# Three pairs' attention scores in row tile 7 instead of 5, and a reordered load queue in row tile 3

## The chip, the core and the metric

The kernel runs on one core of one Trainium2 chip. The core has five instruction queues that run side by side: PE (TensorE, the matrix unit), DVE (VectorE), ACT (ScalarE), POOL (GpSimd) and SP (SyncE, which here only issues DMAs). They meet through semaphores. Matmul results go to PSUM, an accumulator memory of eight banks, from which DVE and ACT read. The metric is device microseconds (us) of one execution; less is better.

## The reference

Inputs q, k and v have 8 batches, 8 heads, 576 positions and 64 values per head. The first half is a retention layer: attention without softmax, with a causal decay that depends on the head.

```
gamma_h = 1 - 2 ** (-5 - h)
ret = (q @ k.T / sqrt(64)) * (gamma_h ** (i - j) where i >= j, else 0)
x   = (ret @ v), heads side by side        # 4608 rows x 512
```

The second half is a two-layer feed-forward on these 4608 rows:

```
h   = x @ w_in                             # 512 -> 2048
g   = h * cos(h)
out = g @ w_out                            # 2048 -> 512
```

## The kernel before

**Pairs and tiles.** The 4608 rows are cut into 18 *pairs* of 256 rows (numbered G) for the retention, and into ten *row tiles* (numbered n) for the feed-forward: one of 512 rows, two of 256, then seven of 512. From tile 3 on (`S7 = 3`) tile n reads the retention results of pairs 2n-2 and 2n-1. The retention of later pairs is laid between the matmuls of the current tile, so that PE always has something to do.

**Retention of one pair.** The decay is split into a factor on q and one on k, applied when they are cast to bf16: `prep_q` and `prep_k` (line 179; `quad` calls `prep_q` four times), nearly always on POOL. `turn_q` and `turn_k` (line 205) then transpose the results by a DMA that SP issues; `turned`, `turned_q` call them. v is only cast: `values` on ACT (line 816) or in `early` on POOL. On PE a pair has five groups of matmuls, 64 x 64 x 64 each from pair 6 on:

- *scores* (`scores`, line 286): 32 matmuls kT x qT, into banks "a"; DVE multiplies them by the causal mask (line 298) and writes `ret`
- *cross* and *same* (line 469, out<-qT,sb): 16 each, the queries times the running state of all earlier positions
- *own* (line 469, out<-ret,vb): 32, the masked scores times v
- *states* (`states`, line 359): k times v; DVE adds them to the running state (lines 380, 382), ACT casts it (lines 390, 391)

cross, own and same add into the same PSUM bank, from which ACT and DVE copy the rows x, transposed, to `xT` (line 494). cross and own use other rows of the matrix unit on the same bank, so after cross a switch is put: `run("cross", True)` appends `nc.scalar.nop()`, an empty instruction on ACT that waits for the last cross matmul, and the first own matmul waits for it.

**A row tile from 3 on** has two halves. In the first, `mm1` (line 545) makes h in eight blocks, ACT takes the cosine (line 553) and DVE the product g (line 554). In the second, `mm2_seven` makes the output with seven products of half-size blocks in the place of eight (the Strassen-like scheme), in the order x = 3, 4, 5, 2, 1, 7, 6, each of 16 matmuls of 128 x 128 x 256 (line 697). Five of the products need sums of parts of g, `g_sum` (line 624), which `sums_after` and `late_sums` hand to DVE or POOL. A POOL sum that follows a DVE sum waits for it. Results are added on DVE (line 722), copied by ACT (lines 742, 747, 752) and stored by `store` (line 729), which then calls `feed`: it issues the next loads and preparations.

**Where the retention sits.** `mm2_seven(n, at)` runs `at[x]` ahead of product x. There are two arrangements:

- tiles 3, 4 and 5, three places: ahead of 5, scores and states of the next pair (`at_once(*ready(G))`); ahead of 1, `unit(G)`: cross of G, scores of G+1, own and same of G, states of G+1; ahead of 6, `begin(G + 1)` and `end(both)`: cross, own and same of G+1 with nothing between. In tile 5 the last place is a `unit` too, which takes the scores and states of the pair after that: three pairs' scores in one tile.
- tiles 6 and 7, two places: a `unit` ahead of 4 and one ahead of 1.

So tiles 3 to 5 take their pairs' scores in the tile itself, and from the end of tile 5 on they are taken one place ahead. Tile 8 ends the retention; tile 9 has none.

**Order.** The program order of each queue is the order in which the Python code emits (the schedule is manual), and each queue runs in that order: what stands behind a waiting instruction waits as well. SP issues nearly all loads, transposes and stores through one queue. Around the change, `feed` in tile 3 is called by the stores of that tile: with r = 0 after the first (`c12`), r = 1 after the second (`c21`), r = 2 and r = 3 after the last two. The first is emitted ahead of product 2, the second ahead of product 1.

Of the kernel before, what the change touches and what calls it, by code (L numbers as in the profile page):

```python
# [17 lines left out]
def kernel(  # L18
# [39 lines left out]
    assert sum(widths) == NTOK  # L58
    starts = [sum(widths[:n]) for n in range(len(widths))]
    S7 = 3  # L60
    LD = 3

    consts = ctx.enter_context(tc.tile_pool(name="consts", bufs=1))
# [346 lines left out]
    def retention(G, bank="m", evac=nc.scalar.copy):  # L410
# [52 lines left out]
        def run(name, switch=False):  # L463
            i = None
            for h, x, yq, n, lhsT, rhs in parts.pop(name):
                at = (x, h % 2)
                left[at] -= 1
                dst = outs[x][half(h % 2), yq, h // 2, :n]
                i = nc.tensor.matmul(  # L469
                    dst if name == "own" else as_queries(G, dst),  # L470
                    lhsT=lhsT,
                    rhs=rhs,
                    start=at not in begun,
                    stop=left[at] == 0,
                    skip_group_check=True,
                )
                begun.add(at)
                if turn:
                    fence(i, turn.pop(), "other rows")
            if switch and i is not None:  # L480
                turn.append(nc.scalar.nop())
                fence(turn[0], i, "other rows")

        def done(*evacs):
# [121 lines left out]
    def g_sum(n, x, e0, e1):  # L606

        gT = tiles["g", n]
        a, b, op_ = {
            5: ((0, 0), (0, 1), ALU.add),  # L610
            2: ((1, 0), (1, 1), ALU.add),
            1: ((0, 0), (1, 1), ALU.add),
            7: ((0, 1), (1, 1), ALU.subtract),
            6: ((1, 0), (0, 0), ALU.subtract),
        }[x]
        if ("gs", n, x) not in tiles:
            tiles["gs", n, x] = sump.tile([P, E2, 256], BF16, tag=f"gs{x}", name=f"gs{x}")
        i0, i1 = (
            gT[:, k * E2 + e0 : k * E2 + e1, r * 256 : (r + 1) * 256] for r, k in (a, b)
        )  # L620
        on_dve = x == 5 or (n, x) == (S7, 2) or (n, x, e0) in (
            (S7, 1, 4), (S7 + 1, 2, 4), (S7 + 2, 2, 4), (last, 1, 0), (last, 2, 4)
        ) or (x == 6 and e0 == 0 and S7 < n < last)
        i = (nc.vector if on_dve else nc.gpsimd).tensor_tensor(  # L624
            out=tiles["gs", n, x][:, e0:e1], in0=i0, in1=i1, op=op_
        )
        if on_dve:
            tiles["gate"] = i
        elif "gate" in tiles:
            fence(i, tiles.pop("gate"), "port free")  # L630

    def sums_after(n, i):

        if n == S7:
            if i < 4:
                w_sums(3 + i % 2, i // 2 * 4, i // 2 * 4 + 4)
            elif i < 6:
                g_sum(n, 5, i % 4 * 4, i % 4 * 4 + 4)
                if i == 5:
                    g_sum(n, 6, 0, 4)  # L640
            elif i == 7:
                g_sum(n, 2, 0, E2)
                g_sum(n, 1, 4, E2)
                g_sum(n, 1, 0, 4)
                for e in (0, 4):
                    g_sum(n, 7, e, e + 4)
                g_sum(n, 6, 4, E2)
        elif n in (S7 + 1, S7 + 2) and i in (3, 7):
            for x in (5, 2):
                g_sum(n, x, i - 3, i + 1)  # L650
            if i == 7:
                g_sum(n, 6, 0, 4)
            g_sum(n, 1, i - 3, i + 1)
            if i == 7:
                for e in (0, 4):
                    g_sum(n, 7, e, e + 4)
                g_sum(n, 6, 4, E2)
        elif i == 3:
            for x in (5, 2, 1, 7) if n < last else (5, 1, 2, 7, 6):
                g_sum(n, x, 0, 4)  # L660
        elif i == 7 and n == last:
            late_sums(n)
# [111 lines left out]

    open_, stores = [], []

    def begin(G, bank="m"):
        run, done = retention(G, bank)
        run("cross", True)
        open_.append(lambda *evacs: (run("own"), run("same"), done(*evacs)))  # L780

    def end(evacs=()):
# [18 lines left out]
    def turned(G):  # L801
        if G < FINE:
            turn_q(G // 2, G % 2)
        turn_k(G)
# [13 lines left out]
    def feed(s):  # L818
# [3 lines left out]
        if n == 0:  # L822
            if r == 0:
                load_q(5)
                load(10)
            elif r == 2:
                quad(4)
                turned_q(4)
                prep_k(8, 0)
                prep_k(8, 1)  # L830
                turned(8)
            elif r == 3:
                prep_k(9, 0)
                prep_k(9, 1)
                turned(9)
                values(8)
                values(9)
            return
# [216 lines left out]
    for n, w in enumerate(widths):  # L1055
# [66 lines left out]
            ]  # L1122
        else:
            at = {}
            if n in (3, 4, 5):
                at = {
                    5: lambda acts, flush, later: (flush(), at_once(*ready(G))),
                    1: lambda acts, flush, later: unit(G, acts, flush),
                    6: lambda acts, flush, later: (flush(), begin(G + 1), end(both)),
                }  # L1130
                if n == 5:
                    at[6] = lambda acts, flush, later: unit(
                        G + 1, acts, flush, lambda masks, add, copy: (masks[0](), add(), copy())
                    )
# [62 lines left out]
```

## Time and profile before

| what | value |
|---|---|
| median of 4 runs | 297.25 us (294.71, 295.07, 299.43, 299.59) |
| the profiled execution, its own time | 294.71 us |
| its span, first to last instruction | 292.9 us |
| PE busy | 279.0 us (95%) |
| DVE, POOL, ACT busy | 207.6, 182.6, 148.9 us |
| granted TensorE clock | 1.00 in every stage |
| DMA, bytes moved | 50.39 MB |

The profile is that of one execution. An engine's busy time says how much it did, not whether it set the end; for that the chain of work that ended last is followed back from the last instruction, and it runs on PE for 88% of the span. In these answers "issue" is time in which an engine waited for nothing that the profile shows. PE's matmuls overlap and their ends are modelled, so durations of stages are taken from starts: from the first matmul of one stage to the first of the next.

### The profile page before, as it was taken

Reading aid. Unit: us, or ns where it says so; the run is one execution under the profiler, and the core shown is the slowest. Engines: PE = TensorE matmul, PEld = TensorE weight load, DVE = VectorE, ACT = ScalarE, POOL = GpSimd, SP = SyncE. Lnnn points to the kernel's source line nnn. Section 1 sums busy time; section 2 is a strip of 40 time slices with the busy share of each in tenths; the row PEclk is TensorE's granted clock in tenths of the full one; section 3 lists DMA queues with packets and bytes.
Section 4 is the critical chain, followed back from the end, with each engine's and each line's share of the span. In section 5 each row is a group of like instructions: output and inputs, shape, how many; then the busy total and the mean of one; then the engine's idle time right before and its main releaser. Section 6 shows DMA issues by size and latency. Waiting matters only on the chain.

```text
span 292.9 us, 8814 instructions
## 1 busy us (share of the span) xinstructions
PE 279.0 (95%) x3822; PEld 192.5 (66%) x3845; DVE 207.6 (71%) x267; ACT 148.9 (51%) x198; POOL 182.6 (62%) x160
## 2 busy tenths in 40 slices
PE   7779999999999999999999979999999999999995
PEld 2658745847658887458745865488548844884594
DVE  6665765494848988589758976788479848945873
ACT  5446614634426636664466436756474657525620
POOL 7890038571194269997686694399949914860583
PEclk9999999999999999999999999999999999999999
DMA  7999999999999999998999999919992240021013
GB/s 223 267 173 190 220 261 242 179 284 239 202 207 209 212 207 232 216 191 192 199 223 224 209 217 223 195 25 258 225 216 41 74 110 0 4 96 50 0 38 108
DMA packets 119031, 50.39 MB, mean 172 GB/s; under 512 B 83024, under 2 KB 117968, under 8 KB 118992
## 3 DMA queue, kind: packets, MB, share of 16 engines
q1 hardware_dynamic: 114224, 45.10, 75.8%
q0 software_dynamic: 4224, 4.19, 9.0%
q8 instruction: 30, 0.49, 0.7%
q10 hardware_dynamic: 544, 0.52, 0.5%
q14 instruction: 9, 0.07, 0.1%
HBM read 36.70 MB, written 9.44 MB: 158 GB/s over the span
## 4 chain that ended last, share of the span: by engine, by line
PE 88%; DVE 6%; issue 2%; ACT 2%; POOL 1%; DVEq 0%; ACTq 0%; POOLq 0%
PE h L545 42%; PE o L697 27%; PE o L562 9%; PE ov L469 4%; PE sc L286 2%; PE st L359 2%; PE tr L985 1%; DVE ret L302 1%; DVE xT L494 1%; DVE ot L722 1%; DVE s L382 1%; ACT kT L241 1%; ACT sb L391 0%; DVE ret L298 0%; DVE qs L974 0%
## 5 line engine op out<-in xcount | busy, mean ns | idle before, releaser
L624 POOL TENSOR_TENSOR gs<-gT 128x1024 bf16<-128x1024 bf16 x44 | 92.4, 2131 | 60.2 <-DVE gs L624 33.5
L545 PE MATMUL h<-xT,w_in_sb 128*128 128x256 bf16 (+1 forms) x756 | 126.7, 325 | 2.2 <-DVE xT L494 1.3
L554 DVE TENSOR_TENSOR gT<-h,cosh 128x1024 bf16<-128x1024 f32 x72 | 87.9, 1223 | 46.9 <-ACT cosh L553 46.5
L553 ACT ACTIVATE cosh<-h,half_pi 128x1024 f32<-128x1024 f32 x72 | 80.2, 1114 | 56.1 <-PE h L545 56.1
L545 PEld LDWEIGHTS <-w_in_sb 128*128 128x128 bf16 x768 | 74.5, 98 | 51.7 <-DVE xT L494 1.8
L697 PEld LDWEIGHTS <-gs 128*128 128x128 bf16 x576 | 53.8, 98 | 6.9 <-POOL gs L624 0.2
L179 POOL TENSOR_TENSOR qs<-fq,gq 128x512 bf16<-128x512 f32 x31 | 31.7, 1056 | 31.6 <-DMA fq<-in_q_dram 31.6
L179 POOL TENSOR_TENSOR ks<-fk,gk 128x512 bf16<-128x512 f32 x34 | 36.7, 1097 | 5.9 <-DMA fk<-in_k_dram 5.8
L697 PE MATMUL o<-ws,gs 128*128 128x256 bf16 (+1 forms) x352 | 38.7, 268 | 0.0
L562 PE MATMUL o<-w_out_sb,gT 128*128 128x512 bf16 x117 | 28.2, 379 | 1.1 <-issue 0.9
L494 ACT CAST xT<-ov 128x512 bf16<-128x512 f32 x28 | 16.3, 622 | 19.4 <-PE ov L469 19.3
L697 PE MATMUL o<-w_out_sb,gT 128*128 128x256 bf16 x224 | 26.1, 273 | 0.0
L722 DVE TENSOR_TENSOR ot<-o,ot 128x512 f32<-128x512 f32 (+2 forms) x32 | 19.6, 619 | 8.7 <-PE o L697 8.2
L697 PE MATMUL o<-w_out_sb,gs 128*128 128x256 bf16 x224 | 25.8, 273 | 0.0
L390 ACT CAST sb<-s 128x768 bf16<-128x768 f32 (+2 forms) x16 | 10.7, 672 | 28.8 <-DVE s L382 26.4
L697 PEld LDWEIGHTS <-gT 128*128 128x128 bf16 x224 | 21.6, 98 | 4.0
L624 DVE TENSOR_TENSOR gs<-gT 128x1024 bf16<-128x1024 bf16 (+1 forms) x25 | 21.3, 883 | 0.4
L562 PEld LDWEIGHTS <-gT 128*128 128x128 bf16 x128 | 11.5, 98 | 12.2
L722 DVE TENSOR_TENSOR ot<-ot,o 128x512 f32<-128x512 f32 x14 | 9.6, 685 | 7.4 <-ACT ot L752 6.2
L298 DVE TENSOR_TENSOR ret<-sc,tri 128x1024 bf16<-128x1024 f32 x12 | 14.6, 1213 | 0.0
L302 DVE TENSOR_TENSOR ret<-sc,tri 128x1024 bf16<-128x1024 f32 x10 | 11.9, 1218 | 2.7 <-PE sc L286 2.6
L469 PE MATMUL ov<-qT,sb 64*64 64x64 bf16 (+1 forms) x424 | 11.2, 201 | 1.2 <-ACT sb L391 0.8
(86 smaller groups left out, 194.4 us busy)
## 6 DMA issues: line engine op xcount, KB each, us to landing
out_dram<-ot SPq DMA_DIRECT2D x35, 256.0 KB, 4.0
fk<-in_k_dram SPq DMA_DIRECT2D x23, 256.0 KB, 6.8
fv<-in_v_dram SPq DMA_DIRECT2D x23, 256.0 KB, 5.2
fk<-in_k_dram SPq DMA_DIRECT2D x4, 512.0 KB, 7.6
fv<-in_v_dram SPq DMA_DIRECT2D x4, 512.0 KB, 7.4
w_in_sb<-in_moe_w_in_dram POOLq DMA_DIRECT2D x4, 512.0 KB, 6.3
w_out_sb<-in_moe_w_out_dram POOLq DMA_DIRECT2D x4, 512.0 KB, 14.1
fq<-in_q_dram SPq DMA_DIRECT2D x4, 512.0 KB, 6.9
```

The lines of the kernel that those rows point to most:

```text
L179: eng.tensor_tensor(out=out_.rearrange("p (b a) d -> p a b d", a=2), in0=f.rearrange("p (a b) d -> p a b d", a=2), in1=by.rearrange("p (a ...
L298: nc.vector.tensor_tensor(out=ret, in0=ps, in1=by, op=ALU.mult)
L302: nc.vector.tensor_tensor(out=ret.rearrange(shape, r=2), in0=ps.rearrange(shape, r=2), in1=by.unsqueeze(1).to_broadcast([P, H, P]), op=ALU ...
L469: i = nc.tensor.matmul(dst if name == "own" else as_queries(G, dst), lhsT=lhsT, rhs=rhs, start=at not in begun, stop=left[at] == 0, skip_g ...
L494: (evacs or (evac, evac))[x](xT[:, x], ps)
L545: nc.tensor.matmul(ps[:, j, :], lhsT=w_in_sb[:, dg, (et + j) * P : (et + j + 1) * P], rhs=xT[:, dg], start=(dg == 0), stop=(dg == DG - 1),)
L553: nc.scalar.activation(cosh, ps, ACTF.Sin, bias=half_pi, scale=1.0)
L554: nc.vector.tensor_mul(gT[:, et : et + m, c0 : c0 + w], ps, cosh)
L562: nc.tensor.matmul(ps, lhsT=gT[:, et, tsi * P : (tsi + 1) * P], rhs=w_out_sb[:, et, :], start=(et == 0), stop=(et == ET - 1),)
L624: i = (nc.vector if on_dve else nc.gpsimd).tensor_tensor(out=tiles["gs", n, x][:, e0:e1], in0=i0, in1=i1, op=op_)
L697: nc.tensor.matmul(dst[i], lhsT=lhs[:, e, j * P : (j + 1) * P], rhs=rhs[:, e, c0:c1], start=(x in (3, 4, 1, 7) and e == 0 and (i == 0 or l ...
L722: pend.append(lambda: nc.vector.tensor_tensor(out=out_, in0=in0, in1=in1, op=op_))
```

## The change

Tiles 6 and 7 get the three-place arrangement that tiles 3, 4 and 5 had; the tile whose last place is a `unit`, with three pairs' scores, is now 7. The sums of g in these tiles follow: product 2's second half goes to DVE. In all three-place tiles the switch between cross and own in `begin` is a drain of PE itself instead of the empty ACT instruction. And in tile 3's `feed` the load of pair 10 is split: k stays at r = 0, v comes after the second store's transposes, and the preparation of q and k of pair 8 and their transposes move from the third store to the second.

```diff
+    CATCH = 7
...
             if switch and i is not None:
-                turn.append(nc.scalar.nop())
+                turn.append(nc.tensor.drain() if switch == "here" else nc.scalar.nop())
                 fence(turn[0], i, "other rows")
...
         on_dve = x == 5 or (n, x) == (S7, 2) or (n, x, e0) in (
-            (S7, 1, 4), (S7 + 1, 2, 4), (S7 + 2, 2, 4), (last, 1, 0), (last, 2, 4)
-        ) or (x == 6 and e0 == 0 and S7 < n < last)
+            (S7, 1, 4), (last, 1, 0), (last, 2, 4)
+        ) or (x == 2 and e0 == 4 and S7 < n <= CATCH) or (x == 6 and e0 == 0 and S7 < n < last)
...
-        elif n in (S7 + 1, S7 + 2) and i in (3, 7):
+        elif n <= CATCH and i in (3, 7):
...
-    def begin(G, bank="m"):
+    def begin(G, bank="m", switch=True):
         run, done = retention(G, bank)
-        run("cross", True)
+        run("cross", switch)
...
             if r == 0:
                 load_q(5)
-                load(10)
-            elif r == 2:
+                load(10, "k")
+            elif r == 1:
                 quad(4)
                 turned_q(4)
                 prep_k(8, 0)
                 prep_k(8, 1)
                 turned(8)
+                load(10, "v")
...
-            if n in (3, 4, 5):
+            if n <= CATCH:
                 at = {
                     5: lambda acts, flush, later: (flush(), at_once(*ready(G))),
                     1: lambda acts, flush, later: unit(G, acts, flush),
-                    6: lambda acts, flush, later: (flush(), begin(G + 1), end(both)),
+                    6: lambda acts, flush, later: (
+                        flush(), begin(G + 1, switch="here"), end(both)
+                    ),
                 }
-                if n == 5:
+                if n == CATCH:
                     at[6] = lambda acts, flush, later: unit(
                         G + 1, acts, flush, lambda masks, add, copy: (masks[0](), add(), copy())
                     )
```

No instruction on PE is added or lost but the drains. By the instruction streams, SP keeps its DMAs: in tile 3 the order changes from k, v (pair 10), store, store, three transposes, store to k, store, three transposes, v, store, store. POOL loses two sums to DVE, one in tile 6 and one in tile 7, and its order in tile 3 stays as it was.

## The prediction

> **What bounds the kernel now.** I read the page first: PE is busy 279.0 of 292.9 us, so a gain must take time out of PE's stream. Then I asked for PE's waits after 85 us, where the change lies. There is a single one:
>
> ```profile
> PE ov L469 <- issue: 2.1, 1, 2.1
> ```
>
> Everything else from tile 3 to tile 9 is matmul after matmul. So a tile's time is its matmuls plus what it loses when it changes from the feed-forward to the retention and back. The chain of work that ended last, in order of time, gives the starts of the stages:
>
> ```profile
> 130.21 3.51 PE o L697 x32
> ...
> 145.73 0.22 PE h L545
> ...
> 159.54 3.49 PE o L697 x32
> ...
> 172.67 0.30 PE ov L469 x30
> 172.97 2.10 issue
> 175.07 0.29 PE ov L469 x12
> ...
> 177.50 0.22 PE h L545
> ...
> 191.32 1.75 PE o L697 x16
> ...
> 206.19 0.21 PE h L545
> ...
> 220.01 1.75 PE o L697 x16
> ...
> 234.88 0.22 PE h L545
> ```
>
> Columns are start, duration, what. From the first "o" to the next "h" is the second half of a tile, the only half that the change touches. It takes 145.73 - 130.21 = **15.52 us** in tile 4 (three places, 256 retention matmuls), 177.50 - 159.54 = **17.96** in tile 5 (three places, 320 matmuls, and the 2.10 us in which PE waited for nothing the profile shows), 206.19 - 191.32 = **14.87** in tile 6 and 234.88 - 220.01 = **14.87** in tile 7 (two places, 256 matmuls each). The first halves agree: 13.84 us in tile 4 (116.37 to 130.21), 13.82 in tiles 6 and 7.
>
> The windows over these halves say what surrounds them; the last two columns are DMA share and GB/s:
>
> ```profile
> 130.20:145.70 15.50, 15.39 (x354) 13.22 (x352) 12.80 (x20) 7.33 (x13) 10.85 (x7) 1.00 1.10 182
> 159.50:177.50 18.00, 15.90 (x418) 13.75 (x416) 14.79 (x24) 8.08 (x15) 15.51 (x12) 1.00 1.12 226
> 191.30:206.20 14.90, 14.90 (x354) 13.02 (x352) 12.50 (x18) 8.11 (x14) 14.28 (x9) 1.00 0.70 156
> 220.00:234.90 14.90, 14.90 (x354) 13.00 (x352) 12.51 (x18) 8.10 (x14) 14.28 (x9) 1.00 0.22 56
> ```
>
> The clock is 1.00 throughout, DVE and POOL have room, and DMA is saturated in tiles 4 and 5 but nearly idle in tile 7.
>
> **The change, part by part.** *Arrangement.* Tile 5 becomes what tile 4 is: 17.96 to 15.52, **-2.44**. Tile 6 becomes what tile 4 is: 14.87 to 15.52, **+0.65**. Tile 7 becomes what tile 5 was. Whether it inherits the 2.10 us is the main question; without them it takes 17.96 - 2.10 = 15.86, **+0.99**. Sum **-0.80**. The 0.65 are no extra matmuls. From tile 4's timeline, its places take 0.65 (133.73 to 134.38), 1.4 and 0.9 us for 64, 128 and 64 matmuls, against 1.2 twice for 128 in tile 6: one more change of shape, and a wait between cross and own.
>
> *Will the 2.10 us follow?* They lie within the own matmuls, 30 of which are recorded before and 2 after; only the first own matmul has a wait in the instruction stream, the others none, so no engine's result is missing. What is left is PE's own instruction supply. The page has a row for it:
>
> ```profile
> q8 instruction: 30, 0.49, 0.7%
> ```
>
> 30 packets carry 0.49 MB, 16 KB each, and 0.49 MB over PE's 7,692 instructions is 64 bytes for each, so one packet is 256 instructions. 0.7% of 16 engines' 292.9 us is 32.8 us, 1.1 us for a packet. Tile 5's second half holds the most instructions for its time: 320 retention matmuls with their weight loads are 640 instructions, two and a half packets, and they run at some 8.4 ns a matmul (0.27 us for 32). It does so with DMA at 1.12. After the change this crowd stands in tile 7, around 231 us, where DMA is at 0.22. I take the stall as gone, at two chances to one. The Trainium skill, "Runtime: NRT & Kernel Launch", section on instruction fetch mechanics, says that refills come in 16 KiB blocks of 256 instructions, as the row shows, but also that PE's instruction memory holds 2048 instructions and that the crossing is mostly hidden; that speaks against my cause, for so deep a store would not run dry in 640. By it the stall is something else and might go along: the sum would then be 2.10 higher. The page also calls this memory two blocks deep, and no run here settles which.
>
> *Drain for ACT's empty instruction*, at four places (tiles 3 to 6, ahead of product 6). In tile 4 the cross matmuls start at 142.88 and own at 143.31; in a unit, where scores stand between, 16 cross matmuls are followed after 0.26 (167.21 to 167.47). The switch thus costs 0.17 here, and 0.19 in tile 3 (113.50 to 113.95, less 0.26). A drain must still let the last cross matmul end, about 0.2 after its start (mean of one: 196 ns). The best is -0.19 at each of the four, -0.76; the trace has no drain on PE, so the upper bound comes from the nearest row of an emptied PE that starts again, a matmul's 0.2 us more at each, +0.8. The two rows nearest to it (0.17 and a 0.2 us latency) say that it nearly pays itself; I take **-0.1** and keep both ends. The Trainium skill, "PSUM — Partial Sum Buffer", section on engine vs sequencer instructions, says that a drain waits until the engine is wholly idle. By it PE would also lose the weight loads that it runs ahead, and the sum would lie nearer 294.7 than 293.8; no row here shows it.
>
> *Sums.* One POOL sum (2.13 us) becomes a DVE sum (0.88) in each of tiles 6 and 7, and POOL's first-half sum for product 7 moves behind block 7. That is tile 4's order, whose 15.52 contains it: **0**. Cover: the last POOL sum of tile 4 ended at 143.02, product 6 began at 143.9. Without that cover each us late is a us of PE. DVE's xT copy ended at 145.29 and the next h began at 145.73: 0.44 us of slack, inherited by tiles 5 and 6.
>
> *SP in tile 3.* The SP queue before:
>
> ```profile
> 113.16 1.98 SPq L170 DMA_DIRECT2D fk<-in_k_dram  x2
> 115.23 6.28 SPq L170 DMA_DIRECT2D fv<-in_v_dram  x2
> 121.61 1.75 SPq L729 DMA_DIRECT2D out_dram<-ot  x2
> 123.47 3.10 SPq L205 DMA_TRANSPOSE qT<-qs  x2
> 126.66 1.29 SPq L205 DMA_TRANSPOSE kT<-ks  x1
> ```
>
> v of pair 10 holds the queue for 6.28 us; the transposes of pair 8 come behind it, land by about 130 (3.1 to 4.8 us after issue) and are used at 133.64. Their q and k were ready on POOL at 117.5 and 119.6. After the change they go some 2 us sooner, and nobody waited for them: **0**. v then starts near 126 instead of 115: the same back-pressure of about 5 us first holds the store (to 120.3), then come store, transposes and kT (1.2 + 3.1 + 1.3). Its second half lands near 127 + 9.0 = 136; ACT casts it at 137.96. The slack is 2 us, and behind that cast stand ACT's copy of product 2 (139.00) and product 7, which needs that bank at about 141.2: 1.6 us more.
>
> *What is late next.* Before, kT of pairs 14 and 16 land at 198.9 and 227.5 (195.78 + 3.1, 224.50 + 3.0), their scores start at 199.67 and 228.4: 0.8 and 0.9 us of slack. After, scores of 14 move into tile 7 and those of 16 to its end near 231: over 20 and 3 us. The order is thus sturdier against a late DMA.
>
> **Sum.** The profiled execution took 294.71: 292.9 of span and 1.81 around it. 294.71 - 0.80 - 0.1 = **293.8**. The median of the runs shown is 297.25, 2.54 above the profiled one; the others reach 299.59. I forecast 293.8 for the median as well, because two races with under 1 us of slack go; if the scatter stays, it comes on top (rival two).
>
> **The rivals.**
> - *The stall stays*, in tile 7 or elsewhere: 293.8 + 2.1 = **295.9**. For it: no wait explains it, and the crowd of instructions is the same. Against it: DMA at 0.22 there. Chance 0.15.
> - *The scatter stays*: whatever put three runs 0.4 to 4.9 us above the profiled one is not in these tiles. 293.8 + 2.5 = **296.3**, up to 298.7. For it: half the runs lie so. Against: the slack gained. Chance 0.22.
> - *v of pair 10 comes too late* (slower than before). One place: ACT's cast at 137.96. If each transpose is held as v's first half was (5.04 us), v starts at 133 and lands at 142: 4 us past its use, 2.4 past product 7's bank, 293.8 + 2.4 = **296.2**, 1.5 over the profiled time. It decides from 3.6 us late. Against: transposes took 1.3 to 1.7 us each. Chance 0.07.
> - *The arrangement is free*: tile 4's 0.65 come from saturated DMA, not from three places. Then tile 5 takes 14.87 + 0.34, tile 6 14.87, tile 7 15.21: -2.75 + 0 + 0.34 = -2.4, and **292.2**. Against: tile 3 with its three places takes 15.54 as well (100.83 to 116.37). Chance 0.08.
>
> The forecast keeps 0.48. The range goes from the cheap case, 292.2, to near the end of the scatter, 298.4. Every case lies within 2% of 297.25 (291.3 to 303.2), which is about what a measurement of this kernel can tell from no change; beyond it lie only the cheap case with the best drain (0.06) and the late v carried on into later tiles (0.04).
>
> **What would show it.** Right: no "issue" wait of PE near 173; second halves near 15.5, 15.5 and 15.9 in tiles 5, 6, 7; cross to own no longer than now; v of pair 10 landed before ACT's cast. Wrong: a PE wait in tile 7's last place; a PE wait for ACT or for kT in tile 4; second halves of tiles 6 and 7 under 15 us; a cross to own gap over 0.4 us.

## The result, and the profile after

| | executions | median | lowest to highest |
|---|---|---|---|
| before | 64 | 296.91 us | 292.77 to 299.59 |
| after | 43 | 294.11 us | 292.35 to 299.25 |

By the medians the change saves 2.80 us (0.94%). The ratio of comparable executions is **0.9956**, 95% interval 0.9937 to 0.9974. It is nearer to 1 than the medians because it leaves out every execution more than 1.5% above the fastest of its kernel, 26 of 64 of before and 3 of 43 of after, and these long executions are a large part of what the change alters. Either way the kernel is a little faster, and within 2%.

The profiled execution of after took 294.88 us (span 293.2); that of before, which carried the whole prediction, took 294.71 (292.9). Only 12 of the 64 executions of before are as short as that. So the two traces show no gain between them, though they do show what moved. First the waits of PE after 85 us in the kernel after (engine, line, releaser; total, times, longest):

```profile
PE st L360 <- issue: 1.5, 1, 1.5
PE o L698 <- issue: 0.5, 2, 0.3
```

The 2.10 us before the 31st own matmul of tile 5's last place are gone, but there is a wait of the same kind, 1.48 us, earlier in tile 5, ahead of `states` in its `unit`. The chain of work that ended last shows it in place (start, duration, what):

```profile
129.25 3.49 PE o L698 x32
...
145.09 0.21 PE h L546
...
158.90 3.49 PE o L698 x32
...
167.27 0.39 PE ov L470 x47
167.67 1.48 issue
169.15 0.44 PE st L360 x23
...
175.98 0.21 PE h L546
...
189.80 3.51 PE o L698 x32
...
205.24 0.21 PE h L546
...
219.06 3.49 PE o L698 x32
...
232.85 1.64 PE o L698 x14
234.49 0.26 issue
...
235.14 0.21 PE h L546
```

Read as before, from the first "o" to the next "h", the second halves of tiles 4 to 7 now take 15.84, 17.08, 15.44 and 16.08 us; before they took 15.52, 17.96, 14.87 and 14.87. The windows over them (busy time and count of PE, its weight loads, DVE, ACT and POOL, then granted clock, DMA share, GB/s):

```profile
129.20:145.10 15.90, 15.52 (x354) 13.11 (x352) 12.86 (x20) 7.33 (x13) 11.55 (x8) 1.00 1.17 198
158.90:176.00 17.10, 15.49 (x353) 13.23 (x352) 12.80 (x20) 7.34 (x13) 14.62 (x11) 1.00 1.18 237
189.80:205.20 15.40, 15.29 (x353) 13.18 (x352) 12.71 (x20) 7.33 (x13) 12.88 (x9) 1.00 0.76 190
219.10:235.10 16.00, 15.74 (x417) 13.49 (x415) 14.18 (x23) 7.81 (x14) 12.26 (x8) 1.00 0.20 53
```

The work itself moved as the diff says: tile 5 has 353 recorded matmuls in place of 418, tile 7 has 417. PE is busy for 15.49 us in tile 5, so but for the new wait it would be a 15.5 us tile.

SP's queue in tile 3 has the new order, and v of pair 10 (the first load of v at the bottom) starts at 124.07; it was ready 8 us before ACT cast it at 137.00:

```profile
112.11 1.61 SPq L171 DMA_DIRECT2D fk<-in_k_dram  x2
113.82 5.22 SPq L730 DMA_DIRECT2D out_dram<-ot  x1
119.15 3.48 SPq L206 DMA_TRANSPOSE qT<-qs  x2
122.72 1.29 SPq L206 DMA_TRANSPOSE kT<-ks  x1
124.07 1.25 SPq L171 DMA_DIRECT2D fv<-in_v_dram  x2
```

### The profile page after: what moved, and what is told of

The parts are those of the page before. It is cut to its first block, busy times and chain, and to the rows that moved or that the text cites. A ratio compares the mean times of both kernels' runs of the same rounds, so it can differ in the third digit from the quotient of the medians.

```text
span 293.2 us, 8817 instructions
## 1 busy us (share of the span) xinstructions
PE 279.2 (95%) x3822; PEld 191.7 (65%) x3845; DVE 206.8 (71%) x271; ACT 147.3 (50%) x196; POOL 178.2 (61%) x158
## 4 chain that ended last, share of the span: by engine, by line
PE 87%; DVE 5%; POOL 3%; issue 2%; ACT 2%; DVEq 0%; PEldq 0%; POOLq 0%; ACTq 0%
PE h L546 43%; PE o L698 26%; PE o L563 9%; PE ov L470 4%; PE sc L287 2%; PE st L360 2%; POOL tri L933 1%; DVE ot L723 1%; DVE s L383 1%; DVE ret L299 1%; DVE xT L495 1%; ACT ot L753 0%; ACT kT L242 0%; PE tr L223 0%; POOL ks L180 0%
## 5 line engine op out<-in xcount | busy, mean ns | idle before, releaser
L625 POOL TENSOR_TENSOR gs<-gT 128x1024 bf16<-128x1024 bf16 x42 | 88.2, 2130 | 67.4 <-DVE gs L625 37.2
L554 ACT ACTIVATE cosh<-h,half_pi 128x1024 f32<-128x1024 f32 x72 | 80.2, 1114 | 53.2 <-PE h L546 53.2
L180 POOL TENSOR_TENSOR qs<-fq,gq 128x512 bf16<-128x512 f32 x31 | 31.8, 1055 | 31.2 <-DMA fq<-in_q_dram 18.6
L698 PE MATMUL o<-ws,gs 128*128 128x256 bf16 (+1 forms) x352 | 39.4, 268 | 0.5 <-issue 0.5
L180 POOL TENSOR_TENSOR ks<-fk,gk 128x512 bf16<-128x512 f32 x34 | 36.0, 1074 | 4.6 <-DMA fk<-in_k_dram 4.2
L495 ACT CAST xT<-ov 128x512 bf16<-128x512 f32 x26 | 15.4, 626 | 22.4 <-PE ov L470 22.4
L625 DVE TENSOR_TENSOR gs<-gT 128x1024 bf16<-128x1024 bf16 (+1 forms) x27 | 19.7, 766 | 0.4
L495 DVE CAST xT<-ov 128x512 bf16<-128x512 f32 x10 | 7.1, 713 | 7.6 <-PE ov L470 4.6
```

What stands on the lines that cost most here:

```text
L180: eng.tensor_tensor(out=out_.rearrange("p (b a) d -> p a b d", a=2), in0=f.rearrange("p (a b) d -> p a b d", a=2), in1=by.rearrange("p (a ...
L495: (evacs or (evac, evac))[x](xT[:, x], ps)
L554: nc.scalar.activation(cosh, ps, ACTF.Sin, bias=half_pi, scale=1.0)
L625: i = (nc.vector if on_dve else nc.gpsimd).tensor_tensor(out=tiles["gs", n, x][:, e0:e1], in0=i0, in1=i1, op=op_)
L698: nc.tensor.matmul(dst[i], lhsT=lhs[:, e, j * P : (j + 1) * P], rhs=rhs[:, e, c0:c1], start=(x in (3, 4, 1, 7) and e == 0 and (i == 0 or l ...
```

## The experiments

Three questions stood open. What is the wait that the profile can only call "issue"? Which part of the change carries the gain? And what makes one execution of before take 293 us and the next 299? The first theory (A in the expectations) was that the wait is PE's instruction supply: a 16 KB block of 256 instructions (the page's "instruction" queue) arrives late, at a fixed position of PE's instruction stream, and how late varies. Its rival for the scatter (B) was the prediction's own reason, the transposes of k of pairs 14 and 16, which had under 1 us of slack.

The experiments are told by question, not in the order in which they ran. A median of one execution says little. Before is the kernel before, run beside it on the same chip, and the ratio is of comparable executions.

| run | what it is | median (executions) | before | ratio, 95% interval |
|---|---|---|---|---|
| e1 | before once more | 296.80 (12) | 296.64 | 1.0009 (0.9968 to 1.0049) |
| e2 | arrangement and its sums alone | 294.50 (12) | 296.64 | 0.9970 (0.9931 to 1.0010) |
| e3 | drain alone (tiles 3, 4) | 295.37 (12) | 296.64 | 0.9978 (0.9940 to 1.0017) |
| e4 | load order of tile 3 alone | 295.91 (12) | 296.64 | 0.9961 (0.9915 to 1.0007) |
| e9 | after once more | 294.91 (12) | 296.82 | 0.9963 (0.9922 to 1.0004) |
| e11 | after without the drain | 294.64 (12) | 296.82 | 0.9949 (0.9915 to 0.9982) |
| e5, e6 | before, 32 or 16 instructions put in front | 294.74, 295.87 (1 each) | 298.22 | |
| e12 | before, 48 instructions put in front | 296.59 (12) | 296.82 | 0.9998 (0.9941 to 1.0054) |
| e7 | before without stores of tiles 0 to 5 | 294.83 (1) | 298.22 | |
| e13 | before without late loads | 291.58 (1) | 296.60 | |
| e8, e10 | after, but three pairs' scores in tile 6 | 292.94 (5), 293.40 (12) | 298.22, 296.82 | 0.9839 (0.9787 to 0.9891), 0.9925 (0.9891 to 0.9959) |
| e14 | as e8, with the old load order | 293.36 (7) | 296.60 | 0.9908 (0.9874 to 0.9943) |
| e15, e16, e17 | e8 with a PE wait in tile 7 | 299.82, 302.36, 303.50 (4 each) | 297.02 | 1.0118 (1.0020 to 1.0216), 1.0187 (1.0111 to 1.0263), 1.0161 (1.0052 to 1.0270) |
| e18 | e8 with a shorter one | 298.17 (10) | 298.17 | 0.9992 (0.9949 to 1.0036) |

### Which part carries the gain

**e1: the kernel before, unchanged.**

> The kernel before, a second time, for a second trace: the median of its runs (296.91 us) lies 2.2 us above the execution that was profiled first (294.71), so a typical execution must hold 2 us or more that the first trace does not show. Theory A (PE's own instruction supply): the second trace shows waits of PE that no engine's result explains, in the retention matmuls of tiles 3 to 6, of 2 to 4.5 us in all, at other places than 172.97. Theory B (late transposes): it shows PE waiting for a DMA ahead of the scores of pair 14 or 16 in tiles 6 and 7 (0.8 and 0.9 us of slack in the first trace), 1 to 2.5 us in all. Time against the kernel before: 1.000.

It took 296.80, and its profiled execution 296.53. PE waited 3.02 us at exactly the place of the 2.10, after 30 own matmuls of tile 5's last place, and there was no wait for a DMA in tiles 6 and 7:

```profile
175.48 0.26 PE L469 MATMUL ov<-ret,vb 64*64 64x64 bf16 x2 [3.02 <-issue]
```

In the other traces, too, PE waits for no DMA there: the two transposes are late in none. The rival for the scatter has fallen.

**e2: the arrangement and its sums alone** (the last place of tiles 3 to 6 keeps ACT's empty instruction, tile 3 keeps its load order).

```diff
+    CATCH = 7
...
-            if n in (3, 4, 5):
+            if n <= CATCH:
...
-                if n == 5:
+                if n == CATCH:
```

> Only the arrangement: three places in tiles 6 and 7 with their sums, three pairs' scores in tile 7; ACT's empty instruction and the load order of tile 3 as before. Theories A and B: this part carries the gain, median 2 to 2.8 us under the kernel before (ratio of medians 0.990 to 0.993). Rival C (the drain carries it): ratio 1.002, because the arrangement alone costs 0.65 + 0.99 - 0.34 = 1.3 us and takes away a stall that is not always there.

294.50: most of the 2.8 us between the medians is here, though the interval of its ratio, 0.9931 to 1.0010, holds no change as well. Nothing waited in tile 5's last place. But waits of the same kind stood elsewhere, in tile 3 and in tile 6 (timeline of PE: start, duration, line, operation, output and inputs, count, idle time before and what ended it):

```profile
109.43 0.44 PE L470 MATMUL ov<-ret,vb 64*64 64x64 bf16 x31 [1.42 <-issue]
...
199.04 0.32 PE L470 MATMUL ov<-ret,vb 64*64 64x64 bf16 x15 [0.56 <-issue]
```

**e3: the drain alone, in tiles 3 and 4. e11: the change with ACT's empty instruction in place of the drain.**

```diff
-                    6: lambda acts, flush, later: (flush(), begin(G + 1), end(both)),
+                    6: lambda acts, flush, later: (
+                        flush(), begin(G + 1, switch="here"), end(both)
+                    ),
```

> Only the drain in place of ACT's empty instruction in tiles 3 and 4 (the two places of the kernel before). Theories A and B: 0.999 to 1.001, cross to own 0.43 us from first to first as before. Rival C: 0.995 or less, with a gap from cross to own that is shorter by 0.1 us or more.

> The changed kernel with ACT's empty instruction in place of the drain at all four places. By the first traces the gap from cross to own stays within 0.02 us, so 0.0 to 0.2 us more than the changed kernel. Rival C (the drain carries a part of the gain, as the median of its own run, 1.3 us under the kernel before, suggests): 0.8 us more or above.

From the first cross to the first own matmul it takes 0.43, 0.45 and 0.43 us with the drain (in e3 and elsewhere) and 0.42 to 0.45 with ACT's instruction (before, e2, e11). The drain is free and gains nothing, and e11 equals e9 (294.64 and 294.91). What e3 lies under before by median has no place in its trace: tile 5 takes 17.93 us in it, with a wait of 2.06.

**e4: the load order of tile 3 alone. e14: three pairs' scores in tile 6, with the old load order.**

```diff
-                load(10)
-            elif r == 2:
+                load(10, "k")
+            elif r == 1:
...
+                load(10, "v")
```

> Only the load order in tile 3: the next k, then q's and k's transposes, then v. All theories: 0.999 to 1.001, since pair 8's transposes land 3 us before use already and v of pair 10 lands some 2 us before its cast. Rival D (the load order carries the gain, because in a typical execution pair 8's transposes are late): 0.992 to 0.995, and e1's trace shows PE waiting for a DMA at the start of tile 4's scores.

> Three pairs' scores in tile 6 with the load order of tile 3 as before. Theory A: the load order has no part in the time, medians 293.0 to 293.9 as with the new order (292.94 and 293.40). Rival D (the load order carries a part, as the median of its own run, 0.7 us under the kernel before, would allow): 294.0 or more.

e4's interval holds no change, and e14 equals e10, which differs from it in nothing but this order (293.36 and 293.40). So the order gives nothing that a run here can see. e4's tile 4 took 16.40 us in its trace instead of 15.52: three DVE sums ran for 2.92 us in it (1.90 in before), and the chain through DVE's adds to `ret` made PE wait 0.26 before the scores.

By the ratios none of e2, e3 and e4 can be told from before, since all three intervals hold 1. The mean granted clock that comes with each execution tells them apart: in e2 6 of 12 executions ran at 0.998 or above, as 26 of 56 did with the whole change, but only 2 of 12 in e3 and 1 of 12 in e4, as 20 of 122 did in before. What that clock means for the time is told below.

### What the wait is

**e5, e6, e12: before with 16, 8 or 24 matmuls of zeros at the start,** where PE idles. Each is two instructions, a weight load and a matmul, and moves all that follows by 32, 16 or 48 positions. If the wait sits at a position of the stream, it moves back by so many instructions. If it belongs to what the kernel does there, it stays.

```diff
-    warm(psum.tile([P, 512], F32, tag="n", name="idle"), 11)
+    idle = psum.tile([P, 512], F32, tag="n", name="idle")
+    for _ in range(16):                                   # e6: 8, e12: 24
+        nc.tensor.matmul(idle[:, :128], lhsT=zeros[:, :P], rhs=zeros[:, :128], start=True, stop=True)
+    warm(idle, 11)
```

> The kernel before with 16 more matmuls (128 columns of zeros, a bank that nobody reads) at the very start of PE's stream: 32 more instructions ahead of everything. Five executions with three pairs' scores in tile 5 all waited 2.1 to 3.0 us in its last place after 29 or 30 of the 32 own matmuls. Theory A (the wait is the arrival of the next block of PE's instructions, so its place is a place in the stream): the wait moves 16 matmuls up, to after 13 to 15 of the own matmuls, and stays 2 to 3 us long. Theory E (it belongs to the work, to what own reads or to the moment): it stays after 29 or 30.

> The same with 8 more matmuls at the start, 16 instructions. Theory A: the wait comes after 21 to 23 of the 32 own matmuls of tile 5's last place, 2 to 3 us long. Theory E: after 29 or 30.

> The kernel before with 24 more matmuls at the start, 48 instructions: nothing of the work moves, only the block boundaries, by 48 instructions. Theory A: in tile 5's last place the wait comes after 5 to 7 own matmuls; tile 4's boundary moves from products 1 and 7 into the end of its unit, tile 3's from own back into scores. The time shifts by up to 3 us either way at equal work, most likely 1 to 3 us less than the kernel before, since the crowded stretch of tile 4 is then cut in two. If it is within 0.3 us of the kernel before, where the boundaries lie does not matter.

The first expectation counts five executions; the traces with three pairs' scores in tile 5 were four by then (before, e1, e3, e4), with waits of 2.06 to 3.02 us.

One line of PE's timeline from each of three kernels, with the wait at its end; the count is that of the own matmuls left after it. Before:

```profile
175.07 0.22 PE L469 MATMUL ov<-ret,vb 64*64 64x64 bf16 x2 [2.10 <-issue]
```

e5, with 32 instructions in front:

```profile
174.88 0.34 PE L469 MATMUL ov<-ret,vb 64*64 64x64 bf16 x18 [2.76 <-issue]
```

e12, with 48:

```profile
175.32 0.58 PE L469 MATMUL ov<-ret,vb 64*64 64x64 bf16 x26 [3.24 <-issue]
```

Of 32 own matmuls, 2 are left without extra instructions, 18 with 32 of them, 26 with 48. That is two instructions for each matmul, and the wait moves with the stream to the instruction. In e6 the boundary stands after 22 own weight loads, as the count of 16 says, but is only 0.20 us long there; instead PE waited 2.76 us in tile 4, three matmuls into product 1. The boundaries lie one block apart. In the traces of e9 to e18 no record of PE is missing. Counted in them, every wait of PE over 0.15 us that no other engine ended stands, to within one instruction, at number 1986, 2753, 3778, 4545, 4802, 5314, 5569 or 6594 of its stream, and the steps between these, 767, 1025, 767, 257, 512, 255 and 1025, are multiples of 256 to within one. Number 4802 is the one in tile 5's last place. The wait is **shown to be the arrival of an instruction block** (a *block wait* from here on).

e12 was meant to gain 1 to 3 us, and did not: 296.59. Moving the boundary 24 matmuls forward, but still among the own matmuls, left the wait.

**e7: before without the stores of tiles 0 to 5** (those rows of the output are left out). **e13: before without the loads of q, k and v after pair 12** (the later pairs compute on pair 12's data).

```diff
+            if n > 5:                                     # e7
+                nc.sync.dma_start(out[r0 : r0 + 256, ...], t)
...
+        if G > 12:                                        # e13; the same for the quad loads of q
+            for name in names:
+                tiles["f" + name, G] = tiles["f" + name, 12]
+            return
```

> The kernel before without the stores of row tiles 0 to 5 (those rows of the output are left out): 5.2 of 50.4 MB less for the DMA engines, so that their share in tile 5's second half falls from 1.12 towards 0.8. If the wait in tile 5 is instructions that stand in line behind data (theory A with saturated DMA): it falls under 1 us, at the same place. If a block takes its time whatever the DMA load (A without contention): 2 to 3 us, at the same place.

> The kernel before, three pairs' scores in tile 5, but without the loads of q, k and v after pair 12 (later pairs work on pair 12's data, so the later rows of the output are other numbers). From about 150 us on only stores and transposes are left, so the DMA share in tile 5's second half falls from 1.12 to some 0.4. PE's instructions, their order and their blocks are unchanged. Theory A with contention (a block of instructions waits in line behind saturated data DMA): the wait in tile 5's last place, after 30 own matmuls, falls under 0.4 us, as in the changed kernel's tile 7 with the same crowd at a share of 0.22 (0.26 to 0.30 us). Theory A without contention (a block takes its time whatever the load): 2 to 3 us at the same place.

e7 told little: the loads closed up into the room, and the DMA share was still 1.08 from 164 to 170 us. PE waited 0.57 us in tile 5's last place and 2.01 us in tile 4. e13 is clear. In the window over tile 5 DMA falls from 1.13 to 0.31, PE has no gap in 18 us, and after 85 us no wait of any kind is recorded:

```profile
159.00:177.00 18.00, 18.00 (x427) 14.54 (x425) 14.94 (x25) 9.56 (x17) 15.51 (x12) 1.00 0.31 81
```

Its tile 5 took 15.67 us in place of 17.96, with the same crowd of 640 retention instructions, and it took 291.58 us in all, 5 under before. So the crowd alone does not make PE wait. Behind the same crowd in tile 7 of after, with DMA at 0.20, PE waits for 0.26 us.

e13 is one execution, though, and e6 with its 0.20 us shows that a block can be nearly in time with saturated DMA as well. The packets settle it. Each trace has all 30 of them with their times. In before, one runs from 172.45 to 173.74, within the wait, and PE goes on 1.33 us after its end; in all 20 traces every block wait of 0.2 us and more ends 1.3 to 1.7 us after the end of a packet. Ahead of the waits over 0.3 us that packet starts only after PE has passed the block boundary before, so PE then has no more than one block in hand. Counted from that boundary, the packet for tile 5's last place started after 4.3 us in before, 5.0 in e1 and 5.3 in e12, and in none of the 19 traces with saturated DMA there after less than 3.0; in e13 it started after 1.4. The packet itself took 0.93 us in e13 and 1.15 to 1.51 in the others. **The block is late where the DMA engines are saturated with data, and mainly because its transfer starts late.**

The Trainium skill ("Runtime: NRT & Kernel Launch", section on instruction fetch mechanics) calls the crossing of such a boundary mostly hidden; e13 agrees, while before, with 2.10 and 3.02 us at one crossing, does not.

### What the scatter is

**The clock.** e1's tile 5 took 20.28 us against 17.96, but its wait was only 0.92 us longer. The other 1.4 us show in the windows behind the wait. The two windows that follow it in before:

```profile
175.40:177.40 2.00, 2.00 (x47) 1.77 (x34) 1.49 (x4) 1.23 (x3) 2.00 (x3) 1.00 1.12 304
177.40:179.40 2.00, 1.95 (x10) 0.92 (x10) 0.83 (x2) 1.12 (x3) 1.96 (x2) 1.00 1.18 152
```

The same windows in e1:

```profile
175.40:177.40 2.00, 1.92 (x52) 1.55 (x53) 0.87 (x3) 1.07 (x2) 2.00 (x3) 0.50 0.92 203
177.40:179.40 2.00, 2.00 (x13) 1.46 (x13) 0.88 (x3) 1.14 (x2) 1.79 (x2) 0.70 0.98 304
```

The granted clock, third from the end, is 1.00 in before and 0.50 and then 0.70 in e1. The 16 matmuls of product 6 take 2.88 us (176.27 to 179.15) in place of 1.76. e12, with its 3.24 us, shows the same, 1.25 us of it. After the waits of 1.4 to 2.76 us in before, after, e2 to e9 the clock stayed at 1.00.

Each execution comes with its mean clock, and 3 us at 0.50 take 0.005 off it. So the executions can be sorted by it (all for which a clock is recorded):

| mean clock | before | after | e8, e10, e14 |
|---|---|---|---|
| 0.998 and above | 20, median 294.6 | 26, median 294.1 | 12, median 293.3 |
| 0.99 to 0.997 | 58, median 297.0 | 24, median 294.2 | 10, median 293.3 |
| below 0.99 | 44, median 298.4 | 6, median 295.8 | 2, median 294.1 |

At full clock before and after are 0.5 us apart. A lowered clock is rarer after the change, and where it occurs it mostly costs nothing there. The traces say why: in after and e10 the low clock lies in the start, at 12 to 16 and 16 to 20 us (0.85 and 0.72 in after, 0.82 and 0.75 in e10), while in e1 it also lies in tile 5, on the path that sets the end.

**e15 to e18: a wait of known length where it is quiet.** If a long wait alone lowers the clock, it does so also in tile 7, with DMA nearly idle, and when ACT makes the wait. In the version with three pairs' scores in tile 6, the first matmul of product 7 of tile 7 is made to wait for 4, 6, 9 or 2 copies on ACT, which wait for the last matmul of product 1. Nothing of the computation changes.

```diff
+            if (n, x) == (7, 7) and (e, i) == order[0]:
+                hops = [nc.scalar.copy(zeros, zeros) for _ in range(4)]   # e16: 6, e17: 9, e18: 2
+                fence(hops[0], tiles["before", 7], "stall")
             mm = nc.tensor.matmul(dst[i], ...)
...
+            if (n, x) == (7, 7) and (e, i) == order[0]:
+                fence(mm, hops[-1], "stall")
+        tiles["before", n] = mm
```

> The version with six as the tile of three pairs' scores (e10: 293.4 us), and in tile 7, between products 1 and 7, a wait of PE made by ACT: four copies of 128 x 512 one after the other, by the cast of the same shape (0.57 us each) and the way to ACT and back an estimated 2.7 us. DMA is nearly idle there (0.21 in e10). Both theories expect the same of this one: the granted clock stays at 1.00 after the wait, since waits of 2.10 and 2.76 us left it there, and the time is e10's plus 2.5 to 3 us, 296.2.

> As e15, with six copies: a wait of an estimated 3.8 us. The theory that the length of PE's wait alone lowers the clock (the traces of e1 and e12 show 0.50 after waits of 3.02 and 3.24 us, and matmuls of product 6 at 180 instead of 110 ns): granted clock 0.5 for some 2 to 3 us after the wait, tile 7's second half longer by the wait plus 1.2 to 1.7 us, time 298.3 to 299. The rival, that the low clock belongs to the late instruction block or to the saturated DMA of tile 5: clock 1.00, time 297.2.

> As e15, with nine copies: a wait of an estimated 5.5 us. The theory that the length of the wait alone lowers the clock: 0.5 for about 3 us in every execution, and no further loss than in e16: time 293.4 + 5.5 + 1.5 = 300.4. The rival: clock 1.00, time 298.9.

> As e15, with two copies. In e15 PE's wait came to 3.59 us, because ACT reached the first copy 0.9 us late; each copy took 0.64 us. Two copies fewer make it 3.59 - 1.28 = 2.3 us. The theory that the length of the wait alone lowers the clock, and only near 3 us: clock 1.00 after the wait, the 32 matmuls of products 7 and 6 take 3.5 us again instead of 4.99, tile 7's second half 14.85 + 2.3 = 17.2 us. The rival, that any wait made by ACT between these products lowers it: clock near 0.5 for 2 to 3 us, 18.6 us.

ACT reached its first copy 0.9 us later than I had counted, so e15's wait became 3.59 us. The timeline of PE in e15 has it:

```profile
233.75 5.15 PE L701 MATMUL o<-ws,gs 128*128 128x256 bf16 x32 [3.59 <-ACT zeros L699]
```

The windows of e15 at the end of the wait and behind it:

```profile
232.00:234.00 2.00, 0.25 (x2) 0.19 (x3) 0.24 (x1) 1.63 (x3) 2.00 (x3) 0.85 0.00 0
234.00:236.00 2.00, 2.00 (x11) 1.44 (x10) 0.00 (x0) 0.00 (x0) 0.25 (x1) 0.50 0.27 55
```

DMA is at 0.00 and 0.27, and the clock falls to 0.50 all the same. The 32 matmuls of products 7 and 6 take 4.99 us (233.75 to 238.74) instead of the 3.5 of e10. With waits of 4.89 and 6.84 us (e16, e17) they take 5.17 and 4.90: about 1.5 us more, whatever the length, as the theory had it. The rival, that the low clock belongs to the late block or to the traffic of tile 5, has fallen. The medians lie 1.3 to 2.4 us above e10 plus wait plus low clock (e15: 293.4 + 3.6 + 1.5 = 298.5, measured 299.8); e15 and e16 show further block waits of 0.6 and 1.1 us elsewhere, which is a part of it, and the rest is not explained.

But e18 went against the theory's figure of 3 us. Its wait was 2.29 us, as expected, and the clock fell too. Its line in PE's timeline:

```profile
235.16 5.30 PE L701 MATMUL o<-ws,gs 128*128 128x256 bf16 x32 [2.29 <-ACT zeros L699]
```

The window of e18 behind the wait:

```profile
236.00:238.00 2.00, 2.00 (x11) 1.44 (x10) 0.00 (x0) 0.00 (x0) 0.95 (x1) 0.50 0.04 8
```

Its 32 matmuls took 5.14 us, the same price, and tile 7's second half 18.95, near the 18.6 that the rival of this run expected. In the traces all five waits of 3.02 us and more lowered the clock, and of eight between 2.01 and 2.76 us this one alone did (2.01, 2.04, 2.06, 2.10, 2.30 and twice 2.76 did not). Those seven are all block waits, this one is ACT's. So length parts the block waits after 85 us, somewhere between 2.76 and 3.02 us in these traces, but it isn't the whole rule. One of e18's ten executions had a mean clock of 1.000 and took 296.0 us, so there the same wait seems to have left the clock alone; chance has a part. And in the start the clock fell to 0.50 in ten of the 20 traces, where no wait of PE was longer than 1.8 us. Whether a wait made by ACT has another limit stays open.

The Trainium skill ("TensorE: Matmul & The Clock Gate", section "What's actually happening") has a gate that halves the clock of an idle PE, by a window of some 3.4 us that runs on its own. The 0.50 agrees, and a window that starts anywhere could be the part of chance. The waits of 2.29, 3.02 and 3.24 us that were enough are shorter than the idle window that the page asks for, and there the measurement decides.

### A version that beats both

**e8 and e10: the change with three pairs' scores in tile 6 instead of 7. e9: the change once more beside it.**

```diff
-    CATCH = 7
+    CATCH = 6
```

> The changed kernel with the three pairs' scores in tile 6: tiles 3 to 6 with three places, tile 7 with two as in the kernel before. By the sums of the trace of before tile 6 pays 0.34 for 64 more matmuls and tile 7 wins back 0.65 + 0.34, so 0.6 us less than the changed kernel if no new wait comes: 0.988 to 0.991 of the kernel before by medians. Theory A: tile 6 (DMA share 0.70) brings a wait of 0.5 to 1.5 us in its last place instead, and the time is that of the changed kernel or up to 1 us more.

> Three pairs' scores in tile 6 a second time, now beside the changed kernel. By the sum 0.6 us less than the changed kernel; its first median, 292.94, says 1.2 us less. Under theory A it has the same boundaries in tiles 3 to 5 as the changed kernel, so nothing more is to be won than tile 7's arrangement: 0.3 to 1.0 us less than the changed kernel. If it is the same within 0.3 us, the arrangement of tile 7 is free.

> The changed kernel a second time, beside the next three on one chip and for a second trace. Theory A: no wait in tile 5's last place; waits of 0 to 2.8 us at the block boundaries that stay in a crowded stretch (in tile 3's unit after the first own matmul, in tile 4 after 11 matmuls of products 1 and 7, in tile 5's unit after the first state matmul). Time 0.990 of the kernel before by medians.

e10 took 293.40, e9 294.91, before 296.82 beside them. Tile 7 goes back to two places (14.85 us in e10, 16.12 in e9), tile 6 takes on the third pair (16.02 and 15.40): 0.65 us by that sum. The rest of the 1.5 us would be the boundary in tile 5 (17.07 us in e9, 15.41 in e10), if these two traces stand for the other executions. Moving the three pairs renumbers nothing ahead of tile 6, so the wait that cost 1.47 us in e9 could have come here as well, but in e10 it did not:

```profile
PE h L546 <- DVE xT L495: 0.6, 1, 0.6
PE o L698 <- issue: 0.2, 1, 0.2
PE sc L287 <- issue: 0.2, 1, 0.2
```

e8's trace has a wait of 2.04 us in tile 4. So how late a block comes is decided anew in each execution, and I can't say that e10's place is safer for tile 5. What is shown: all 24 executions of this version (e8, e10, and e14 with the old load order) lie between 292.5 and 295.0, where after's lie between 292.4 and 299.3, and in e9 up to 300.7. Tiles 6 and 7 of e10:

```profile
188.70:204.70 16.00, 15.80 (x418) 13.70 (x416) 14.22 (x23) 7.82 (x14) 13.48 (x10) 1.00 0.75 183
218.60:233.40 14.80, 14.80 (x353) 12.98 (x352) 12.47 (x18) 8.10 (x14) 14.17 (x9) 1.00 0.21 56
```

Second halves, first "o" to next "h", from the timelines of PE (us; the chain above rounds after's by 0.01 otherwise):

| | tile 3 | tile 4 | tile 5 | tile 6 | tile 7 | sum | rest of the span |
|---|---|---|---|---|---|---|---|
| before | 15.54 | 15.52 | 17.96 | 14.88 | 14.88 | 78.8 | 214.1 |
| e1, before again | 15.54 | 15.77 | 20.28 | 14.88 | 14.88 | 81.4 | 213.3 |
| after | 15.81 | 15.83 | 17.08 | 15.45 | 16.08 | 80.2 | 213.0 |
| e9, after again | 15.76 | 15.84 | 17.07 | 15.40 | 16.12 | 80.2 | 214.2 |
| e11, after, no drain | 15.48 | 15.94 | 15.44 | 15.39 | 15.83 | 78.1 | 214.4 |
| e10, scores in tile 6 | 15.80 | 15.81 | 15.41 | 16.02 | 14.85 | 77.9 | 213.6 |
| e13, no late loads | 15.87 | 15.52 | 15.67 | 14.86 | 14.87 | 76.8 | 212.9 |

The rest of the span varies by 1.5 us, these five halves by 4.6, and most of that is tile 5 with its block boundary.

## Why the prediction was right or wrong

**Right: the direction, and where the work goes.** Tile 6 was to take 15.52 and took 15.45 (15.39 and 15.40 in e11 and e9; 16.12 in e2, which has a block wait of 0.56 there); tile 7 without the stall was to take 15.86 and took 16.08, of which 0.26 is a block wait. Tile 5 without a wait is 15.44 in e11, where 15.52 was forecast. The rival "arrangement is free" is thereby wrong: the 0.6 and 1 us of tiles 6 and 7 came, with DMA at 0.76 and 0.20.

**Right, and now shown: PE's instruction supply.** The guess from the page's row of 30 packets holds, down to 256 instructions (e5, e12), and a block comes late where DMA is saturated (e13 and the starts of the packets). The stall was gone from its place and did not follow into tile 7, as taken at two to one. What I had missed is that the boundary exists every 256 instructions. Tile 5 has another, in its `unit`, and in the traces of after and e9 it cost 1.48 and 1.47 us there. So the rival "the stall stays, in tile 7 or elsewhere", at 0.15, came true in part in these two executions, though not in e11's. The term of tile 5, -2.44, was thus -0.88 in after's trace against the profiled before, but -2.52 in e11's. It is not one number but a draw.

**Mis-sized: the drain,** -0.1 with bounds of -0.76 and +0.8: 0.0 (e3, e11). Three drains stand in before's trace, too, but at its start and end (0.32, 288.14 and 292.43 us), where they price nothing. The reorder at 0 stands; v of pair 10 had 8 us of slack where I had 2: the back-pressure fell on a store as forecast, but the load landed 3.7 us after its issue and not the 9.0 of before. The rival "v too late" was far off, and its sum was wrong too: three transposes held for 5.04 us each put the start of v at 136.6 us, not 133. One sign could tell nothing, "a cross to own gap over 0.4 us": from first to first it was 0.43 already in before.

**The step that failed** is the last one: "I forecast 293.8 for the median as well, because two races with under 1 us of slack go". The sum was -0.9 us on a profiled execution of 294.71, a ratio of 0.997. The comparable executions gave 0.9956, -1.3 us, with the sum's 0.997 just inside the interval. On top of that I promised the median 2.5 us more, from 297.25 to 293.8, or 1.16% where the ratio is 0.44%. The medians did go from 296.91 to 294.11, close to what I wrote, but by luck, since the reason given was wrong. The two transposes were late in no trace. What kept executions of before above the profiled one is, by e1's trace, the very wait that I had read as 2.10 us: it was 3.02 there, followed by some 3 us at half clock, 2.3 us more in tile 5 for the two together. That PE's clock could fall after a wait was nowhere in the sum, because the one profile I read showed 1.00 throughout. The rival "the scatter stays" was wrong too by the medians, and right by what the ratio compares.

That the change removes these executions by moving the boundary out of tile 5's last place fits all traces. With three pairs' scores in tile 5 and nothing else moved, PE waited 2.06 to 3.02 us there (before, e1, e3, e4); in the 11 traces with them in tile 6 or 7, in whose stream the same boundary falls on the first matmuls of tile 6, it waited 1.15 us in e18 and at most 0.19 in the others. For the executions without a trace it is argued from the table of clocks and from e2, which alone brings 2.1 of the 2.8 us. Open is why a block's transfer starts 3 us after the boundary in one execution and 5 in the next.

## What to carry to other kernels

An "issue" wait of PE in a dense stretch of small matmuls can be a late instruction block: shift the stream by some dummy instructions at the start, and if the wait moves by as many, it is one; then put the dense stretch where the DMA engines are idle, or thin out the transfers there. The times of the 16 KB packets in the DMA records say the same without a change of the kernel. Price a PE wait of 2 us and more with the half clock that can follow it, here 1.3 to 1.7 us. And where executions of one kernel scatter by 2%, sort them by their mean granted clock before attributing the difference to any part of a change.

## What the hardware showed that I had not expected

- A wait of PE can cost more than its length. After waits of 3.02 to 6.84 us the granted clock was 0.50 for some 3 us, and the matmuls behind took 1.25 to 1.66 us more; one wait of 2.29 us, made by ACT, had the same price, while seven block waits of 2.01 to 2.76 us had none. In the start of ten traces the clock fell with no wait over 1.8 us.
- Instruction blocks of 16 KB compete with data. At a DMA share of 1.1 PE waited up to 3.2 us for one, at 0.2 to 0.3 between 0 and 0.3 us. The packet for tile 5's last place took 0.93 us in e13 and 1.15 to 1.51 in the other traces, but started 3.0 to 5.4 us after the boundary before in place of 1.4.
- A drain on PE costs no more than an empty instruction on ACT that PE waits for: 0.43 to 0.45 us against 0.42 to 0.45 from cross to own.
- The same three DVE sums took 1.90 us in before and after, 2.92 in e4 and 2.75 in e2; why is not shown.
